# Column-tiled transposes and denominator sums, and a searched order with a lead for dense work, in a two-layer attention and MLP kernel

## The chip, the core and the metric

The kernel runs on one core of a Trainium2 chip. The core has five engines with an instruction stream each: PE (matrix products, from SBUF into PSUM), ACT (activations), DVE and POOL (elementwise work), SP (here it only issues transfers). They meet through semaphores alone. The metric is the device time of one execution in microseconds (us). Times "before" are the median of 8 runs.

## What is computed

Four blocks in a row, each with its input added to its output: attention A, mixer and MLP B, attention A, mixer and MLP B. Both A use the same weights, and so do both B. There are 2048 tokens of 512 values in bf16. Attention has 32 heads of 16 values, which share one key and one value head. Cut to what matters:

```python
def _A_ref(x, wq, wk, wv, wo):            # x: (1, 2048, 512), H = 32, Dh = 16
    q = (x @ wq).reshape(B, S, H, Dh).transpose(0, 2, 1, 3)
    k = x @ wk
    v = x @ wv
    p = softmax(einsum("bhqd,bkd->bhqk", q, k) * Dh ** -0.5)
    o = einsum("bhqk,bkd->bhqd", p, v)
    return o.transpose(0, 2, 1, 3).reshape(B, S, H * Dh) @ wo

def _B_ref(x, w1, w2, w3, w4):            # w3: (512, 1792), w4: (1792, 512)
    h = gelu(layernorm(x) @ w1)
    # the four quarters of h are moved along the tokens by +1, -1, +2, -2
    x1 = x + shifted(h) @ w2
    return x1 + gelu(layernorm(x1) @ w3) @ w4

x = A_x
x = x + _A_ref(layernorm(x), ...)
x = x + _B_ref(layernorm(x), ...)
x = x + _A_ref(layernorm(x), ...)
x = x + _B_ref(layernorm(x), ...)
```

## The kernel before

The tokens are 16 tiles of 128. A layer (A and B together) takes them in chunks of four tiles as queries; the last four of layer 1 are two chunks of two. A chunk's attention is eight blocks `b` of four heads, a block is 16 key tiles `kb`, and each of these is cut into two halves of two heads. With the two short chunks counted in steps of two key tiles, a layer has 1024 such halves, of 128 x 1024 scores each.

**Halves and their two ways.** PE forms the scores (L1072, QT and KT, on array tiles of 32 rows, one for each head). Then either ACT takes the exponential (L1116, `declare_unit`: 1024 columns from two PSUM banks into EA; two such slots of banks take turns), or the half is "given" to DVE and POOL (`declare_pair`): DVE turns the scores into the bits of a bf16 power of two (L1137, J), and two further integer additions (L1147, JK, on POOL or DVE) give three terms whose weighted sum approximates the exponential. PE adds EA @ VP, or three products with J, JK and the scaled VD, in one PSUM bank ACC (L1196, `declare_pv`). A column of ones in VP collects the denominators.

**The end of a block** (`block_end`): DVE copies ACC to ACCF (L1230); PE picks the denominators out of it with SELC (L1238, `fz`: 128 x 128 of ACCF against 4 columns, four times for 512 queries), DVE takes reciprocals (L1245), PE spreads them with IDENT (L1253, `fx`), DVE multiplies (L1259, OS), and SP moves the result to OT in eight transfers (L1282).

**The end of a chunk** (`chunk_end`): output projection (`outproj`), layer norms with rows in ZR, transposes of 128 x 128 on PE (L868, `across`; then one copy at L877), first mixer product (`mixer_in`) with its gelu on ACT (L1457, GP), second (`mix`), the MLP's first product (`mlp`, copies at L1532) with its gelu (L1537, G), and its second (`mlp_out`). A tile whose mixing needs tokens of the next chunk is left to that chunk, so MLP groups of layer 0 are tiles 0-2, 3-6, 7-10, 11-13 and 14-15. At the passage from layer 0 to 1 each finished tile gives keys and values of layer 1 (`kv`), on which the first chunk of layer 1 waits; it therefore takes the key tiles in three stretches (below 6, below 11, the rest).

**What sets the order.** Nothing here is a loop over engines. `Plan` is a list scheduler that runs while the program is built: each operation has a duration, a priority and its inputs, and `run` places operations on model times; `emit` writes the resulting order, with semaphore waits, into the program. On the chip every engine follows that order. Side work (all that is not attention) is released no faster than `PACE` allows: an operation's `ready` is at least its `entry`, which moves on by each operation's PE time. `MARGIN` is what the planner adds when PE waits for another engine. `SWITCH` is what it charges when PE changes among three kinds of work: "Q" (scores, 32-row tiles), "P" (32-column tiles) and "F" (full array: transposes, `fz`, values). `filler` puts products of ONES and NIL on PE when its activity in a window is low. `assign` decides when a half is given to DVE and POOL.

Eight of the planner's numbers (`RULES`) change along the way: each stretch of 12.5 us takes one of 16 rows of `MOODS`, and the string `TEMPER` names the row of each stretch. It has been found by a search over built orders.

Of the kernel before, what the change touches and what calls it, by code (L numbers as in the profile page):

```python
# [25 lines left out]

class Op:
    __slots__ = ("eng", "emit", "preds", "npend", "succ", "dur", "prio", "seq", "ready", "start",
                 "end", "take", "give", "dma", "out", "pos", "sem", "vc", "side", "placed", "pe", "feeds", "port", "parts", "after")


class Plan:
# [6 lines left out]

    DRAIN = {"ACT": 0.15, "DVE": 0.085, "POOL": 0.0}  # L40
    SELF = 0.035
    MARGIN = 0.09
    SWITCH = 0.103
    WAVE = 0.006
    WINDOW = 3.4133
# [2 lines left out]
    KEEP = 0.55  # L48
# [8 lines left out]
    PATIENCE = 3.0  # L57
    SLACK = -0.1
    DMA_LATE = 2.5
    NEAR_FILL = 0  # L60
    STICK = -1
    CLOSE = 2.5
# [38 lines left out]
    def op(self, eng, emit, reads=(), writes=(), dur=0.1, prio=None, take=None, give=None,  # L101
           dma=0, out=False, side=True, pe=None, port=False, parts=1, after=0.0):
        o = Op()
        o.eng, o.emit, o.dur, o.take, o.give, o.dma, o.out, o.side = \
            eng, emit, dur, take, give, dma, out, side
        o.pe = pe
        o.port = port
        o.parts = parts
        o.after = after
        o.feeds = None  # L110
        o.seq = len(self.ops)
        o.prio = self.base if prio is None else prio
        o.succ = []
        o.placed = False
        o.start = o.end = None
        o.pos = None
        preds = set()
        for t in reads:
            r = self.res.get(t)
            if r is not None and r[0] is not None:  # L120
                preds.add(r[0])
        for t in writes:
            r = self.res.get(t)
            if r is not None:
                if r[0] is not None:
                    preds.add(r[0])
                preds.update(r[1])
        for t in reads:
            self.res.setdefault(t, [None, []])[1].append(o)
        for t in writes:  # L130
            self.res[t] = [o, []]
        o.preds = preds
        for t in writes:
            if isinstance(t, Late):
                if take is None:
                    t.gates += [p for p in preds if p not in t.ops]
                t.ops.append(o)
        o.ready = self.now
        if self.pace is not None and side:
            if pe is not None:  # L140
                self.release += pe[1] * self.pace / 2400.0
                if take is not None:
                    self.entry = self.release
            o.ready = max(o.ready, self.entry)
        n = 0
        for p in preds:
            if p.placed:
                o.ready = max(o.ready, self._after(p, o))
            else:
                p.succ.append(o)  # L150
                n += 1
        o.npend = n
        self.ops.append(o)
        self.left += 1
        if n == 0:
            self._push(o)
        return o
# [35 lines left out]

    def _push(self, o):
        self.heap[o.eng].append(o)
        heapq.heappush(self.events, o.ready)

    def _pick(self, eng, t, dense=False):
# [13 lines left out]
        best = None  # L212
        bank = None
        for o in h:
            if o.ready > t + 1e-9:
                continue
            if eng == "ACT" and self.closing and o.side and not all(u.placed for u in self.units[-4:]):
                continue
            if joins and (o.pe[0] != self.pe_kind or self.begin(o, t) > t + 1e-9):
                continue  # L220
            if limit and o.prio > 0:
                end = self.run_end(o, t)
                if (not joins or end > self.pe_end + 0.02) and \
                        any(end + (self.SWITCH if o.pe[0] != "Q" else 0.0) > x for x in limit):
                    continue
            if pressing and self.run_end(o, t) > self.pe_end + 0.02:
                continue
            key = (low.get(o, o.prio), o.seq)
            if self.CLOSE and eng == "PE" and o.prio > 2 and o not in low and o.take is None:
                key = (self.CLOSE, o.seq)  # L230
            if stick and o.prio > 2 and o.pe[0] == self.pe_kind and not any(self.run_end(o, t) + self.SWITCH > x for x in due):
                key = (self.STICK, o.seq)
            if o in pinned:
                key = (self.PINNED, o.seq)
            if best is not None and key > best[0]:
                continue
            k = None
            if o.take is not None:
                if not all(p.placed and (p.end <= t + 1e-9 or p.eng == "PE") for p in o.take.gates):
                    continue  # L240
                margin = self.MARGIN if o.side else self.LAT["PE"]
                for i, (ft, b) in enumerate(self.pool):
                    if ft + margin <= t + 1e-9 and (k is None or ft < self.pool[k][0]):
                        k = i
                if k is None or o.prio > 2 and len(self.pool) <= self.SPARE and self.attach is not None and not self.loose:
                    continue
            best = (key, o)
            bank = k
        if best is None:
            return None  # L250
        o = best[1]
# [65 lines left out]
        return self.free_at["DVE"] - self.now + sum(o.dur for o in self.heap["DVE"] if o.prio <= 2)  # L317

    def backlog(self):
        return sum(o.dur for o in self.heap["DVE"] if o.side and o.ready <= self.now + 0.5)  # L320

    def _place(self, o, t):
        o.start = t
        o.placed = True
        if o.port and o.eng == "POOL" and o.dur > 0.5:
            x = self.order["DVE"][-1] if self.order["DVE"] else None
# [3 lines left out]
        o.pos = len(self.order[o.eng])  # L330
        self.order[o.eng].append(o)
        if o.dma:
            s = max(t + 0.61 * (o.parts - 1) + 1.4, self.dma_free)
            o.end = s + o.dma / 330e3 + 0.6
            self.dma_free = s + o.dma / 330e3
            self.free_at[o.eng] = t + 0.63 * o.parts
        elif o.eng == "PE":
            self.roll(t)
            kind, stream, act = o.pe[0:3]
# [2 lines left out]
            end = t + stream / f + (self.WAVE * ((stream + 511) // 512) if kind == "P" else 0.0)  # L342
# [170 lines left out]
def mm(n, k=1):  # L513
    return ("F", max(n, 60) * k, n * k)


def tiled(n, k=1):
    return ("P", n * k, n * k, range(4))
# [6 lines left out]
class Kernel:  # L525
# [16 lines left out]
    ADDS = 4  # L542
# [10 lines left out]
    MAX_PAIRS = 2  # L553
    BACKLOG = 1
    FAR = 20
    FREE = 2
    LONELY = 3
    SOON = 0.45
    QUEUE = 0.7

    STRETCH = 12.5
    RULES = ("KEEP", "PATIENCE", "BACKLOG", "LONELY", "SOON", "QUEUE", "MAX_PAIRS", "ADDS")
    MOODS = (
        (0.55, 3.0, 1.0, 3.0, 0.45, 0.7, 2, 4),
        (0.53, 2.5, 0.8, 3.0, 0.45, 0.7, 2, 5),
        (0.57, 3.5, 1.2, 3.3, 0.45, 0.7, 2, 4),
        (0.52, 3.0, 1.5, 2.0, 0.6, 0.7, 2, 5),
        (0.55, 2.0, 1.0, 3.0, 0.3, 1.0, 2, 4),
        (0.55, 4.0, 0.7, 4.0, 0.45, 0.5, 2, 4),
        (0.55, 3.0, 1.0, 3.0, 0.45, 0.7, 1, 4),  # L570
        (0.55, 3.0, 1.5, 2.5, 0.6, 1.0, 3, 5),
        (0.60, 3.0, 0.6, 3.0, 0.2, 0.4, 2, 4),
        (0.50, 2.7, 1.1, 2.8, 0.5, 0.8, 2, 4),
        (0.55, 3.0, 2.0, 1.5, 0.45, 0.7, 2, 3),
        (0.55, 1.0, 1.0, 3.0, 0.45, 0.7, 2, 4),
        (0.55, 3.0, 1.0, 3.0, 0.45, 0.7, 2, 5),
        (0.55, 3.0, 1.0, 3.0, 0.45, 0.7, 2, 3),
        (0.55, 3.0, 1.5, 3.0, 0.7, 1.2, 3, 6),
        (0.57, 2.0, 1.0, 2.0, 0.45, 1.0, 3, 4),
    )  # L580
    TEMPER = "8033ee39ee377177e2fc0e03ec3fe7470c0ad17fee0e5df7ee7330e00050000a42037e4ce5591f07513f43f3fee2df192097e373cc00f03c4"

    def __init__(self, nc, ins, out):
        self.stretch = -1
# [271 lines left out]
    def across(self, tiles, dst, dtags, base=None, prio=None, eng="DVE"):  # L856
# [5 lines left out]
        for hd in range(2):  # L862
            def fpe(e, hd=hd):
                ins = None
                for dc in (2 * hd, 2 * hd + 1):
                    for i, tb in enumerate(tiles):
                        x = (dc * n + i) * 128
                        ins = e.transpose(self.PBH[:, L.bank, x:x + 128], rows[:, tb % 4, dc * 128:(dc + 1) * 128],  # L868
                                          self.IDENT)
                return ins  # L870
            op("PE", fpe, reads=[(name, tb % 4) for tb in tiles] + [("ID",)], writes=[L], pe=mm(128, 2 * n),
               prio=prio, take=L if hd == 0 else None)
        src = lambda: self.shaped(self.PBH[:, L.bank, 0:512 * n], [4, n * 128])
        if eng == "ACT":
# [329 lines left out]
    def block_end(self, la, c, b, end):  # L1204
# [30 lines left out]
        def fz(e):  # L1235
            ins = None
            for q in range(nq):
                ins = e.matmul(self.PB[:, L.bank, 4 * q:4 * q + 4], lhsT=acc[:, q * 128:(q + 1) * 128],  # L1238
                               rhs=self.SELC, start=True, stop=True)
            return ins  # L1240
        op("PE", fz, reads=am + [("SELC",)], writes=[L], pe=("F", 60 * nq, 4 * nq), prio=fin, take=L)

        def frec(e):
            with self.nc.allow_low_precision("the reciprocals feed a bf16 matmul"):
# [359 lines left out]
```

## Time and profile before

| | |
|---|---|
| median of 8 runs (lowest, highest) | 1501.86 us (1501.41, 1502.61) |
| the profiled execution | 1501.62 us, of which span 1499.8 us |
| granted clock of PE | 1.000 |
| exponentials on ACT (L1116) | 1430, 1315.7 us busy |
| halves on DVE and POOL | 618 (1236 J of 681 ns; JK: 1014 on POOL, 222 on DVE) |
| transposes (L868) | 384 |
| denominator products (L1238) | 256 |
| filler matmuls (ONES, NIL, L671) | 636 of 396 ns, four of them side by side |
| ACT table loads | 30 of 1.283 us |
| weight and input transfers | 7.9 MB read; queues busy 4.9% of 16 engines |

A row of the groups gives line, engine, operation, what is written from what, the count, busy time and mean length, and after the second bar the engine's idle time before such instructions with what ended it. [...]what a matmul costs its engine is read from the distance of the starts in the timeline. PE's 98% is such a sum of overlapping records, not a measure of how much of PE is used.

### The profile page before, as it was taken

To read this page: it belongs to the slowest core of one execution; us is meant where nothing else is said; L and a number is where in the kernel's file an instruction comes from. 1 tells how busy PE (TensorE), PEld (TensorE's weight loads), DVE (VectorE), ACT (ScalarE), POOL (GpSimd) and SP (SyncE) were. 2 spreads that over 40 slices of the span, in tenths; PEclk is the share of its full clock that TensorE was granted. 3 is DMA by queue.
4 is the path that set the end of the run, shared out by engine and by line. 5 is a ranking of instruction groups with operands and counts; after the bars stand their busy time and mean duration, and the time that the engine had idled before them with its cause. 6 is when DMAs were issued, how large, how long until landed. Compare 5 with 4: busy or idle time off the path is not lost.

```text
span 1499.8 us, 62760 instructions
## 1 busy us (share of the span) xinstructions
PE 1476.8 (98%) x28277; PEld 653.8 (44%) x28277; DVE 1327.5 (89%) x2397; ACT 1429.3 (95%) x1520; POOL 1210.9 (81%) x1275
## 2 busy tenths in 40 slices
PE   9999999999999999999999999999999999999999
PEld 4343343444443444444354334344443344555565
DVE  8999999998999999999886799998799998988973
ACT  7999999999999999999959999999999999999952
POOL 2999999997998887998833799889889898887941
PEclk9999999999999999999999999999999999999999
DMA  6100100001000000100000000010000000000000
GB/s 213 29 7 4 20 6 6 6 4 20 7 6 4 6 5 6 19 4 2 2 3 3 2 7 13 6 19 5 13 14 6 6 6 13 6 19 10 9 14 24
DMA packets 32141, 21.49 MB, mean 14 GB/s; under 512 B 12672, under 2 KB 31360, under 8 KB 31872
## 3 DMA queue, kind: packets, MB, share of 16 engines
q1 hardware_dynamic: 31872, 17.47, 4.9%
q8 instruction: 221, 3.62, 1.0%
q14 instruction: 48, 0.39, 0.1%
HBM read 7.90 MB, written 2.10 MB: 7 GB/s over the span
## 4 chain that ended last, share of the span: by engine, by line
ACT 71%; PE 24%; DVE 3%; POOL 1%; issue 0%; DMA 0%; POOLq 0%
ACT EA L1116 68%; PE PB L671 10%; PE PB L1072 6%; PE PB L1196 6%; ACT G L1537 1%; DVE J L1137 1%; POOL JK L1147 1%; ACT L1116 1%; PE PB L868 1%; ACT GP L1457 1%; DVE JK L1147 0%; PE PB L925 0%; ACT L1457 0%; ACT L1537 0%; DVE ST L786 0%; DVE G L1532 0%
## 5 line engine op out<-in xcount | busy, mean ns | idle before, releaser
L1116 ACT ACTIVATE EA<-PB 128x1024 bf16<-128x1024 f32 x1430 | 1315.7, 1150 | 5.4 <-PE PB L1072 3.1
L1147 POOL TENSOR_SCALAR JK<-J 128x1024 uint16<-128x1024 uint16 x1014 | 1074.3, 1060 | 169.0 <-DVE J L1137 84.5
L1137 DVE TENSOR_SCALAR J<-PB 128x512 uint16<-128x512 f32 x1236 | 794.5, 681 | 75.2 <-PE PB L1072 70.3
L1072 PE MATMUL PB<-QT,KT 32*128 32x512 bf16 (+1 forms) x4608 | 610.2, 359 | 13.1 <-ACT EA L1116 6.2
L1196 PE MATMUL PB<-EA,VP 128*32 128x256 bf16 (+1 forms) x6448 | 370.0, 263 | 1.4 <-DVE ACCF L1230 1.0
L1072 PEld LDWEIGHTS PB<-QT,KT 32*128 32x128 bf16 x4608 | 163.0, 91 | 377.3 <-ACT EA L1116 301.0
L1196 PE MATMUL PB<-JK,VD 128*32 128x256 bf16 (+1 forms) x5536 | 318.2, 266 | 2.2 <-POOL JK L1147 1.1
L1196 PEld LDWEIGHTS PB<-EA,VP 128*32 128x32 bf16 x6448 | 154.7, 95 | 121.2 <-issue 93.9
L1196 PEld LDWEIGHTS PB<-JK,VD 128*32 128x32 bf16 x5536 | 126.7, 94 | 149.1 <-issue 93.0
L1196 PE MATMUL PB<-J,VD 128*32 128x256 bf16 (+1 forms) x2768 | 175.3, 264 | 0.2 <-DVE J L1137 0.2
L671 PE MATMUL PB<-ZT,W 128*32 128x512 bf16 (+2 forms) x2816 | 167.6, 342 | 0.7 <-DVE J L1137 0.2
L1147 DVE TENSOR_SCALAR JK<-J 128x1024 uint16<-128x1024 uint16 x222 | 141.4, 643 | 3.2 <-PE PB L1196 1.0
L671 PE MATMUL PB<-W,G 128*32 128x512 bf16 x1624 | 103.0, 380 | 0.1
L1196 PEld LDWEIGHTS PB<-J,VD 128*32 128x32 bf16 x2768 | 67.8, 95 | 42.1 <-issue 34.3
L1532 DVE CAST G<-PB 128x512 bf16<-128x512 f32 (+2 forms) x126 | 71.9, 580 | 15.3 <-PE PB L671 14.3
L671 PEld LDWEIGHTS PB<-ZT,W 128*32 128x32 bf16 x2816 | 65.0, 96 | 33.1 <-issue 16.8
L1537 ACT ACTIVATE G<-G 128x1792 bf16<-128x1792 bf16 x29 | 47.0, 1686 | 32.7 <-DVE G L1532 32.6
L806 POOL TENSOR_TENSOR SM<-SM,MH 128x2 f32<-128x2 f32 (+1 forms) x69 | 49.1, 715 | 21.2 <-DVE SM L808 10.0
L671 PE MATMUL PB<-ONES,NIL 128*32 128x512 bf16 x636 | 57.8, 396 | 0.1
L671 PEld LDWEIGHTS PB<-W,G 128*32 128x32 bf16 x1624 | 41.3, 96 | 34.4 <-issue 9.2
L1259 DVE TENSOR_TENSOR OS<-ACCF,PB 128x512 bf16<-128x512 bf16 (+1 forms) x72 | 44.6, 620 | 7.5 <-PE PB L1253 7.4
L1513 POOL TENSOR_TENSOR X<-Y,X 128x512 f32<-128x512 bf16 x32 | 37.6, 1180 | 9.7 <-DVE Y L1495 7.8
(108 smaller groups left out, 837.0 us busy)
## 6 DMA issues: line engine op xcount, KB each, us to landing
OT<-OS SPq DMA_DIRECT2D x424, 8.0 KB, 1.8
W<-in_B_w_dram SPq DMA_DIRECT2D x2, 1792.0 KB, 14.5
X<-in_A_x_dram SPq DMA_DIRECT2D x8, 256.0 KB, 4.9
QT<-QS SPq DMA_DIRECT2D x32, 64.0 KB, 2.4
out_dram<-OUTB SPq DMA_DIRECT2D x16, 128.0 KB, 1.7
OT<-OS SPq DMA_DIRECT2D x104, 4.0 KB, 2.2
W<-in_B_w_dram SPq DMA_DIRECT2D x2, 512.0 KB, 8.9
WQ<-in_A_wq_dram SPq DMA_DIRECT2D x1, 512.0 KB, 4.4
```

Source lines behind the costliest of these rows:

```text
L671: ins = e.matmul(self.PB[32 * g:32 * g + 32, bank, 0:n], lhsT=lhsT[:, 32 * g:32 * g + 32], rhs=rhs, start=start, stop=stop, tile_position= ...
L806: op("POOL", lambda e: e.tensor_tensor(out=out, in0=src, in1=self.MH[:, 0, a:b], op=ALU.pow), reads=tags + [("MH",)], writes=tg(r), dur=0. ...
L868: ins = e.transpose(self.PBH[:, L.bank, x:x + 128], rows[:, tb % 4, dc * 128:(dc + 1) * 128], self.IDENT)
L1072: ins = e.matmul(self.PB[:, bank, j * n:(j + 1) * n], lhsT=self.KT[32 * h:32 * h + 32, la, (kb + j) * 128:(kb + j + 1) * 128], rhs=self.QT ...
L1116: o = q.feeds = op("ACT", lambda e: e.activation(self.EA[:, ea, :, :], self.PB[:, b0:b0 + 2, :], ACTF.Exp, scale=0.25), writes=bk + [("EA" ...
L1137: o = op("DVE", lambda e, i=i, L=L: e.tensor_scalar(out=J[:, i * 512:(i + 1) * 512], in0=self.PB[:, L.bank, :], scalar1=128 * LOG2E * 0.25 ...
L1147: x = op(eng, lambda e, k=k, r=r: e.tensor_scalar(out=self.JK[:, r, :], in0=J, scalar1=float(self.STEPS[k]), scalar2=1.0, op0=ALU.add, op1 ...
L1196: ins = e.matmul(self.PB[32 * x:32 * x + 32, self.ACC, p * hw:p * hw + hw], lhsT=v[:, la, kb + j, :], rhs=ap[:, i, j * w + u * hw:j * w + ...
L1259: op("DVE", lambda e: e.tensor_tensor(out=osm, in0=acc, in1=self.PB[:, M.bank, 0:n], op=ALU.mult), reads=am, writes=[M] + om, dur=t_ps(n), ...
L1513: op("POOL", lambda e, tb=tb: e.tensor_tensor(out=self.X32[:, tb, :], in0=self.Y[:, tb % 6, :], in1=self.X32[:, tb, :], op=ALU.add), reads ...
L1532: op("DVE", lambda e, f=f, L=L: e.tensor_copy(self.G2[:, f, 0:n], self.PB[:, L.bank, 0:n]), writes=[L] + [(x, f, i) for x in ("G2", "GE") ...
L1537: op("ACT", lambda e, i=i: e.activation(self.G2[:, :, i * 128:(i + 1) * 128], self.G2[:, :, i * 128:(i + 1) * 128], ACTF.Gelu_apprx_tanh), ...
```

## The change

- The transposes of `across` and the products of `fz` are issued as four column tiles: each 128-column left operand is cut into four of 32 columns, and each part writes its own 32 PSUM partitions. There are four times as many instructions, and the planner counts them as kind "P", like most other products. `fz` is priced at 100 columns for each 128 queries.
- `entry` leaves `ready`: an operation of the side work can be picked when its `entry` is no more than `EAGER` ahead. `EAGER` is a ninth rule of the table (-15 to 20 us; 0 in most rows), and rows 10 and 13 are changed in other rules too.
- The planner takes 0.7 us for each transfer that SP issues, in place of 0.61 and 0.63.
- `MARGIN` is 0.15, not 0.09.
- `TEMPER` is another string.

```diff
-    MARGIN = 0.09
+    MARGIN = 0.15
...
+    EAGER = 0.0
+    ISSUE = 0.7
...
         o.ready = self.now
+        o.entry = 0.0
         if self.pace is not None and side:
...
-            o.ready = max(o.ready, self.entry)
+            o.entry = self.entry
...
         self.heap[o.eng].append(o)
+        if o.entry > self.now:
+            heapq.heappush(self.events, o.entry)
         heapq.heappush(self.events, o.ready)
...
-            if o.ready > t + 1e-9:
+            if o.ready > t + 1e-9 or o.entry > t + self.EAGER:
...
-        return sum(o.dur for o in self.heap["DVE"] if o.side and o.ready <= self.now + 0.5)
+        return sum(o.dur for o in self.heap["DVE"] if o.side and max(o.ready, o.entry - self.EAGER) <= self.now + 0.5)
...
-            s = max(t + 0.61 * (o.parts - 1) + 1.4, self.dma_free)
+            s = max(t + self.ISSUE * (o.parts - 1) + 1.4, self.dma_free)
...
-            self.free_at[o.eng] = t + 0.63 * o.parts
+            self.free_at[o.eng] = t + self.ISSUE * o.parts
...
-    RULES = ("KEEP", "PATIENCE", "BACKLOG", "LONELY", "SOON", "QUEUE", "MAX_PAIRS", "ADDS")
+    RULES = ("KEEP", "PATIENCE", "BACKLOG", "LONELY", "SOON", "QUEUE", "MAX_PAIRS", "ADDS", "EAGER")
...
-        (0.57, 3.5, 1.2, 3.3, 0.45, 0.7, 2, 4),
-        (0.52, 3.0, 1.5, 2.0, 0.6, 0.7, 2, 5),
...
-        (0.55, 3.0, 2.0, 1.5, 0.45, 0.7, 2, 3),
+        (0.57, 3.5, 1.2, 3.3, 0.45, 0.7, 2, 4, 8.0),
+        (0.52, 3.0, 1.5, 2.0, 0.6, 0.7, 2, 5, -6.0),
...
+        (0.55, 3.0, 1.0, 3.0, 0.45, 0.7, 2, 4, 20.0),
...
-    TEMPER = "8033ee39ee377177e2fc0e03ec3fe7470c0ad17fee0e5df7ee7330e00050000a42037e4ce5591f07513f43f3fee2df192097e373cc00f03c4"
+    TEMPER = "0004c7ec07f77e4f907027ef07eeee79fc406e0770e7473e37722cc100f0b580559f773c3777120e4e54ee2fe471e1217c7e4070c38e21c731"
...
-                        ins = e.transpose(self.PBH[:, L.bank, x:x + 128], rows[:, tb % 4, dc * 128:(dc + 1) * 128],
-                                          self.IDENT)
+                        for g in range(4):
+                            y = dc * 128 + 32 * g
+                            ins = e.transpose(self.PBH[32 * g:32 * g + 32, L.bank, x:x + 128],
+                                              rows[:, tb % 4, y:y + 32], self.IDENT, tile_position=(0, 32 * g))
                 return ins
-            op("PE", fpe, reads=[(name, tb % 4) for tb in tiles] + [("ID",)], writes=[L], pe=mm(128, 2 * n),
+            op("PE", fpe, reads=[(name, tb % 4) for tb in tiles] + [("ID",)], writes=[L], pe=tiled(128, 2 * n),
...
-                ins = e.matmul(self.PB[:, L.bank, 4 * q:4 * q + 4], lhsT=acc[:, q * 128:(q + 1) * 128],
-                               rhs=self.SELC, start=True, stop=True)
+                for g in range(4):
+                    y = q * 128 + 32 * g
+                    ins = e.matmul(self.PB[32 * g:32 * g + 32, L.bank, 4 * q:4 * q + 4], lhsT=acc[:, y:y + 32],
+                                   rhs=self.SELC, start=True, stop=True, tile_position=(0, 32 * g))
             return ins
-        op("PE", fz, reads=am + [("SELC",)], writes=[L], pe=("F", 60 * nq, 4 * nq), prio=fin, take=L)
+        op("PE", fz, reads=am + [("SELC",)], writes=[L], pe=("P", 100 * nq, 4 * nq, range(4)), prio=fin, take=L)
```

## The prediction

> **What bounds the kernel now.** Read first the busy times and the chain of waits on the page: ACT is the last engine for 71% of the span, PE for 24%, and no transfer is in the chain.
>
> ```profile
> PE 1476.8 (98%) x28277; PEld 653.8 (44%) x28277; DVE 1327.5 (89%) x2397; ACT 1429.3 (95%) x1520; POOL 1210.9 (81%) x1275
> ACT 71%; PE 24%; DVE 3%; POOL 1%; issue 0%; DMA 0%; POOLq 0%
> ```
>
> ACT was busy 1429.3 of 1499.8 us, so only 70.5 us of its time can be won without giving it less work. The second view is the timeline of ACT alone, which shows where those 70.5 us lie. Its columns are start, length, instruction, and in brackets the idle time before it with its cause.
>
> ```profile
> 33.97 201.77 ACT L1116 ACTIVATE EA<-PB 128x1024 bf16<-128x1024 f32 x220 [0.62 <-PE PB L1072]
> ...
> 754.00 1.91 ACT L1457 ACTIVATE GP<-GP 128x2048 bf16<-128x2048 bf16 x1
> ...
> 759.55 6.46 ACT L1537 ACTIVATE G<-G 128x1792 bf16<-128x1792 bf16 x4
> ...
> 786.22 4.87 ACT L1537 ACTIVATE G<-G 128x1792 bf16<-128x1792 bf16 x3 [15.66 <-DVE G L1532]
> ...
> 794.83 10.46 ACT L1116 ACTIVATE EA<-PB 128x1024 bf16<-128x1024 f32 x11 [0.49 <-PE PB L1072]
> 806.80 16.61 ACT L1116 ACTIVATE EA<-PB 128x1024 bf16<-128x1024 f32 x18 [1.52 <-PE PB L1196]
> ```
>
> The first row is what most of the kernel looks like: 220 exponentials in 201.77 us, 0.917 us each, without a gap. The others are the passage from layer 0 to layer 1. There ACT stands 15.66 + 0.49 + 1.52 = 17.7 us. Up to 33.97 us another 7.7 us are lost, and from the last exponential (ended at 1437.06 us) to the end of the span a tail of 62.7 us runs on PE. Everywhere else ACT's gaps sum to about 1 us. So the end can move by four things alone: ACT's work, the head, the passage, the tail. The third view, the timeline of PE in the passage, says why ACT stands.
>
> ```profile
> 758.49 0.39 PE L1072 MATMUL PB<-QT,KT 32*128 32x512 bf16 x2
> 758.80 2.78 PE L671 MATMUL PB<-W,GP 128*32 128x512 bf16 x48
> 761.41 4.92 PE L671 MATMUL PB<-W,G 128*32 128x512 bf16 x88
> ...
> 781.23 4.07 PE L671 MATMUL PB<-ZT,W 128*32 128x384 bf16 x96
> 785.24 0.84 PE L868 MATMUL PB<-IDENT,QS 128*128 128x128 bf16 x12
> ```
>
> After the scores at 758.49 PE writes no scores until 787.94: it works off in one piece what two tile groups left, and ACT has nothing in hand but gelus that wait for it.
>
> **Part 1, the new order (table, lead, planned transfers).** The planner writes each engine's order into the program, so both orders can be counted. The counts: exponentials 1430 to 1433; pairs of score tiles on DVE and POOL 618 to 615; ACT table loads 30 to 28; filler matmuls 636 to 612. Layer 0 has 706 exponentials on ACT in both, with the same gelus and loads, so up to there nothing moves.
> ACT's work: 3 x 0.917 = +2.75 us, and two loads of 1.283 us less (the page's L1116 loads) = -2.57. Sum **+0.2 us**. DVE loses 6 J (681 ns) and 6 JK (643 ns), 8 us off the path.
>
> The passage. Before, ACT's order is: 769 exponentials, the mixer gelu GP, 1 exponential, four MLP gelus (chunk 2), 2 exponentials, three gelus (first part of chunk 3), then 31. After: 748, the four gelus, GP directly behind, 29 exponentials, the three gelus, 36. Chunk 2's first MLP product is done by exponential 747, not 770, and PE's one block becomes two. I price a block from rows: two 512-wide dots are 0.43 us (the 88 matmuls from 761.41 to 766.26 are 11 such: 4.85 us with a switch), two 384-wide 0.325 (the 96 from 781.23 to 785.24 are 12 such: 4.0), a P.V group 0.11, a scores pair with its switch 0.32. As a check, the old block has 6 mix and 28 MLP-out halves (34 x 0.43), 28 halves of 384 (9.1), six transpose ops (1.1), seven P.V groups (0.8) and four switches (0.4): 26.0 us, and the trace has 758.80 to 785.24, 26.4.
> - First new block, behind exponential 750's scores: 0.3 + six P.V 0.66 + 8 mixer halves 3.44 + 18 MLP-out 7.74 + 4 mix 1.72 + 0.4 = 14.3 us, and 0.3 for the next scores. ACT meanwhile has load 1.28, four gelus 6.46, GP 1.91, load 1.28, two exponentials 1.83 = 12.8. ACT stands 1.9 us. GP needs the mixer's casts 5.2 us into the block and comes at 7.7, so it does not wait.
> - Between the blocks 26 exponentials (23.8 us of ACT) have about 23 us of PE work: no gap.
> - Second block, behind exponential 777's scores: 0.32 + 0.33 + 5 MLP-out 2.15 + 22 halves of 384 7.15 + 0.55 for the last cast = 10.5 us; ACT holds two exponentials and a load, 3.1. ACT stands 7.4.
> - The last stretch (fillers, third group) I leave near its old value, 2.0 to 1.3.
> Idle 10.6 for 17.7: **-7.1 us**. Were all PE work pushed against ACT's, without the bank of the gelus, it would be 12.5 (-5); if PE also runs ahead between the blocks, 8.5 (-9).
>
> Waits that the new order adds: behind the four gelus on ACT now stand GP and all exponentials; if GP is late, PE waits for the score banks too. The time from layer 0's last exponential to GP shrinks from 59 to 46 us. Before, POOL's chain for the first two tiles took 717.08 to 725.5, with four JK of 1.04 to 1.23 between its steps; after, its eight steps stand together, so some 4.4 us shorter, and the moved transposes come about 10 us behind the outproj, for a chain of some 7. Enough.
> SP: 626 transfers in both; per issue the trace has 5.92/8 = 0.74 us. The waits view has one wait of DVE for a DMA, 1.5 us at the first load, and none for OT or QT, so planned issue times cost or win nothing by themselves (0 to -1). Out stores and QT copies trade places in layer 1, without a waiter in that view.
>
> **Part 2, transposes and sums in four column tiles.** Runs of one array shape change 3009 times before, 2880 after. One change costs 0.10 us (P.V to P.V 0.12, P.V to scores 0.22 start to start). -129 x 0.10 = -13 us of PE. A transpose op becomes 16 small matmuls of exactly the shape of the L1253 row, which stream as long as four full ones did. For the sums the nearest row is the same:
>
> ```profile
> L1253 PE MATMUL PB<-IDENT,RZ 128*32 128x128 bf16 x1024 | 29.0, 220 | 0.0
> L1238 PE MATMUL PB<-SELC,ACCF 128*128 128x4 bf16 x256 | 17.4, 168 | 0.0
> ```
>
> Sixteen of them ran 403.46 to 403.79, 0.23 us without the switch, 14 ns each. The old sums of four took 0.18 with a switch, 0.08 without. So 64 blocks cost 64 x 0.13 = +8 us. Against it speaks the Trainium skill, TensorEngine Tiling, section Instruction Overhead: about 60 cycles for each matmul however small, and no tiling taken from a dimension that is small already; here it is 4. At the 2.4 GHz that page TensorE: Matmul & The Clock Gate states, that is an estimated 25 ns, 0.40 a block, 64 x 0.32 = +20 us. By the row the part, with 6 fillers fewer (-1.3), gives PE -6 us; by the rule +6. I take the row: same shape, same engine, and it has 0.23, not 0.40. Either lies off the path where ACT has no gap: with shared rows counted once, PE's rows sum to about 0.93 of ACT's time outside the passage, in both orders (at worst 1.02 per 50 exponentials before, 0.97 after), and two exponentials (1.8 us) of score banks hide a block of 0.4. If the cover were gone, -6 to +6 us would show.
> In the tail PE sets the end. After: one MLP half (0.43) and one P.V group (0.11) fewer, five runs of full-array work lose two switches each (0.8 to 1.0), sums +0.06: **-1.3 us** (0 to -2). The head has the same transposes and two fillers more, still before data: 0 (+-0.7).
>
> **Sum.** +0.2 - 7.1 - 1.3 = -8.2: span 1491.6. The profiled execution took 1501.62, 1.8 around its span, and 0.24 under the median: 1491.6 + 1.8 + 0.2 = **1493.6 us**.
>
> **Rivals.**
> 1. The gap stays the same size: the passage is work, not order, and PE's sum there falls only by pairs and switches (7 pairs fewer between exponentials 750 and 800, 3 us). Then +0.2 - 3 - 1 = 1498. For it: PE had no gap from 753 to 785. Against: 11 us of gelus now lie over PE's first block. 0.15.
> 2. The gain is larger: transposes and rearranged stages also clear the head (7.7 us) and the gap before the second block: -14, 1488. Nothing in the head's order says so. 0.12.
> 3. Slower: a producer is late at a moved transpose or at GP. PE works in order, so scores queue behind; beyond 1.8 us of bank ACT stands. Before, POOL's chain with JK between took 14 us from the second tile's outproj to its transpose; after, some chunks leave 10. If the chain stays long, 4 - 1.8 = 2.2 us at each of 9 chunk ends, 20 us: 1493.6 + 20 = 1513; it decides from four ends on. Against: the JK are out of that chain, and the planner leaves 0.15 us where it left 0.09. 0.10.
> 4. The lead and tiles do nothing, the order is a reshuffle: 1501.9, 0.05.
>
> The rest, 0.58, is the forecast. The range takes its bounds and rivals 1 and 2: 1487.5 to 1500.5. From no change a measurement here tells 0.2%, 3 us (1498.9 to 1504.9). Faster 0.81, same 0.08, slower 0.11.
>
> **What would show it.** On ACT's timeline the three gelus' wait falls from 15.66 to 6 to 9, with about 2 us after GP; the last exponential ends near 1430; the tail is 61 us. The L1238 group's blocks start 0.2 to 0.25 apart from what follows; 0.4 would be the rule's price. A wait of ACT for scores, above 1 us and outside the passage, would be rival 3.

## The result, and the profile after

The changed kernel takes 1497.24 us (median of 10 runs, 1496.61 to 1498.63) against 1501.89 us for the kernel before on the same chip: ratio 0.9969, 95% interval 0.9961 to 0.9977. The gain is 4.65 us where 8.3 were forecast. The profiled execution is the longest of the ten, 1498.63 us with a span of 1496.5. A second execution with the same order on PE, ACT, DVE and SP (experiment 3) took 1496.81 us, span 1495.0. It is used beside the first, because it shows how far two executions of one order lie apart.

The page first: two lines that answer to those shown of before.

```profile
PE 1468.2 (98%) x30149; PEld 652.1 (44%) x30149; DVE 1333.3 (89%) x2385; ACT 1429.7 (96%) x1521; POOL 1212.6 (81%) x1275
ACT 61%; PE 30%; DVE 6%; POOL 2%; issue 1%; DMA 0%; SPq 0%
```

ACT has the same work as before (1429.7 for 1429.3 us). PE lost 8.6 us of busy time although it now carries 1872 more matmuls. In the chain of waits PE and DVE gained share, 30 and 6% for 24 and 3: ACT is less alone on the path than it was.

The timeline of ACT alone tells where the time went. Its columns are start, length, instruction, and the idle time before it with its cause.

```profile
9.08 1.01 ACT L882 COPY YT<-PB 128x1024 bf16<-128x1024 bf16 x1 [2.40 <-PE PB L875]
13.23 0.59 ACT L940 CAST KT<-PB 128x512 bf16<-128x512 f32 x1 [3.14 <-PE PB L932]
14.46 5.63 ACT L1123 ACTIVATE EA<-PB 128x1024 bf16<-128x1024 f32 x6 [0.64 <-PE PB L1079]
21.90 5.60 ACT L1123 ACTIVATE EA<-PB 128x1024 bf16<-128x1024 f32 x6 [1.81 <-PE PB L1079]
28.90 6.64 ACT L1123 ACTIVATE EA<-PB 128x1024 bf16<-128x1024 f32 x7 [1.40 <-PE PB L1079]
36.10 212.33 ACT L1123 ACTIVATE EA<-PB 128x1024 bf16<-128x1024 f32 x231 [0.56 <-PE PB L1079]
...
738.76 6.46 ACT L1546 ACTIVATE G<-G 128x1792 bf16<-128x1792 bf16 x4
745.12 1.89 ACT L1466 ACTIVATE GP<-GP 128x2048 bf16<-128x2048 bf16 x1
...
752.59 24.89 ACT L1123 ACTIVATE EA<-PB 128x1024 bf16<-128x1024 f32 x27 [2.33 <-PE PB L1079]
...
787.06 4.87 ACT L1546 ACTIVATE G<-G 128x1792 bf16<-128x1792 bf16 x3 [8.28 <-DVE G L1541]
...
795.60 15.88 ACT L1123 ACTIVATE EA<-PB 128x1024 bf16<-128x1024 f32 x17 [0.42 <-PE PB L1079]
812.52 15.69 ACT L1123 ACTIVATE EA<-PB 128x1024 bf16<-128x1024 f32 x17 [1.03 <-PE PB L1203]
```

In the passage, from 738 us on, the one wait of 15.66 us has become two, 2.33 and 8.28, as the forecast had it (1.9 and 7.4). The new loss is at the top: the waits of 1.81 and 1.40 us at 21.90 and 28.90 stood at 0.56 and 0.38 before. These are the rows of before:

```profile
19.82 7.44 ACT L1116 ACTIVATE EA<-PB 128x1024 bf16<-128x1024 f32 x8 [0.56 <-PE PB L1072]
27.64 5.71 ACT L1116 ACTIVATE EA<-PB 128x1024 bf16<-128x1024 f32 x6 [0.38 <-PE PB L1072]
```

PE's timeline of the kernel after shows both the passage's first block and what happens ahead of those two waits.

```profile
20.41 0.29 PE L875 MATMUL PB<-IDENT,ZR 128*32 128x128 bf16 x6
20.97 0.57 PE L875 MATMUL PB<-IDENT,ZR 128*32 128x128 bf16 x26 [0.28 <-issue]
21.47 0.40 PE L1079 MATMUL PB<-QT,KT 32*128 32x512 bf16 x4
...
26.25 0.61 PE L932 MATMUL PB<-YT,WK 128*32 128x512 bf16 x6
27.72 0.82 PE L932 MATMUL PB<-YT,WK 128*32 128x512 bf16 x10 [0.85 <-issue]
28.47 0.39 PE L1079 MATMUL PB<-QT,KT 32*128 32x512 bf16 x2
...
380.11 0.29 PE L1203 MATMUL PB<-J,VD 128*32 128x256 bf16 x4
380.23 0.25 PE L1247 MATMUL PB<-SELC,ACCF 128*32 128x4 bf16 x16
380.33 0.28 PE L1203 MATMUL PB<-JK,VD 128*32 128x256 bf16 x4
...
738.78 3.63 PE L676 MATMUL PB<-ZT,W 128*32 128x512 bf16 x64
742.23 7.94 PE L676 MATMUL PB<-W,G 128*32 128x512 bf16 x144
750.00 1.90 PE L676 MATMUL PB<-W,GP 128*32 128x512 bf16 x32
```

Twice in the head PE stops in the middle of one operation, after 6 of 32 transposes and after 6 of 16 key products, with "issue" as the cause: no semaphore was awaited. From 738.78 to 751.73 lies the first new block, 64 + 144 + 32 matmuls, eight for each half: the 8 mixer, 18 MLP-out and 4 mix halves that were forecast. The rows at 380 us are read further down.

All of ACT's time adds up to the span, so the account can be closed. Exponentials are the summed lengths of their rows; head is the idle time in rows that start before 40 us, the tail what follows the last exponential.

| us, after less before | forecast | profiled after | same order, second execution |
|---|---|---|---|
| exponentials (1433 for 1430) and two table loads fewer | +0.2 | +3.4 - 2.6 | +2.6 - 2.6 |
| head (7.66 before) | 0 | +3.0 | +2.7 |
| passage (17.67 before) | -7.1 | -5.6 | -5.6 |
| gaps elsewhere (0.95 before) | 0 | 0.0 | -0.4 |
| tail (62.75 before) | -1.3 | -1.45 | -1.4 |
| span | -8.2 | -3.3 | -4.8 |

Two theories for the difference were open. **The fetch theory**: in the head PE's instructions, which come by DMA themselves, arrive late beside the weight loads, because tiled transposes are four times as many instructions. **The order theory**: the new order itself is worse in the head. And a question beside it: which part of the change carries the gain, the tiles, the order, or the lead? The expectations below number their theories each for itself; the text between them uses these names.

### The profile page after: what moved, and what is told of

Its sections match the earlier page's. It is cut to its first block, busy times and chain, and to the rows that moved or that the text cites. A ratio compares the mean times of both kernels' runs of the same rounds, so it can differ in the third digit from the quotient of the medians.

```text
span 1496.5 us, 66501 instructions
## 1 busy us (share of the span) xinstructions
PE 1468.2 (98%) x30149; PEld 652.1 (44%) x30149; DVE 1333.3 (89%) x2385; ACT 1429.7 (96%) x1521; POOL 1212.6 (81%) x1275
## 4 chain that ended last, share of the span: by engine, by line
ACT 61%; PE 30%; DVE 6%; POOL 2%; issue 1%; DMA 0%; SPq 0%
ACT EA L1123 57%; PE PB L1079 10%; PE PB L676 9%; PE PB L1203 9%; DVE J L1144 3%; POOL JK L1154 2%; ACT G L1546 2%; ACT L1123 1%; PE PB L875 1%; DVE ST L791 1%; DVE G L1541 1%; ACT GP L1466 1%; PE PB L932 0%; DMA X<-in_A_x_dram 0%; DVE JK L1154 0%
## 5 line engine op out<-in xcount | busy, mean ns | idle before, releaser
L1123 ACT ACTIVATE EA<-PB 128x1024 bf16<-128x1024 f32 x1433 | 1318.8, 1127 | 9.8 <-PE PB L1079 8.1
L1203 PE MATMUL PB<-EA,VP 128*32 128x256 bf16 (+1 forms) x6460 | 366.3, 263 | 0.7 <-DVE ACCF L1237 0.4
L1203 PE MATMUL PB<-JK,VD 128*32 128x256 bf16 (+1 forms) x5512 | 321.6, 266 | 4.6 <-POOL JK L1154 2.6
L1154 DVE TENSOR_SCALAR JK<-J 128x1024 uint16<-128x1024 uint16 x216 | 152.1, 712 | 2.4 <-PE PB L1203 0.8
L676 PEld LDWEIGHTS PB<-W,G 128*32 128x32 bf16 x1624 | 38.0, 96 | 36.2 <-issue 10.7
L1522 POOL TENSOR_TENSOR X<-Y,X 128x512 f32<-128x512 bf16 x32 | 37.3, 1169 | 11.7 <-DVE Y L1504 10.0
## 6 DMA issues: line engine op xcount, KB each, us to landing
W<-in_B_w_dram SPq DMA_DIRECT2D x2, 1792.0 KB, 14.5
```

The lines of the kernel that those rows point to most:

```text
L676: ins = e.matmul(self.PB[32 * g:32 * g + 32, bank, 0:n], lhsT=lhsT[:, 32 * g:32 * g + 32], rhs=rhs, start=start, stop=stop, tile_position= ...
L1123: o = q.feeds = op("ACT", lambda e: e.activation(self.EA[:, ea, :, :], self.PB[:, b0:b0 + 2, :], ACTF.Exp, scale=0.25), writes=bk + [("EA" ...
L1154: x = op(eng, lambda e, k=k, r=r: e.tensor_scalar(out=self.JK[:, r, :], in0=J, scalar1=float(self.STEPS[k]), scalar2=1.0, op0=ALU.add, op1 ...
L1203: ins = e.matmul(self.PB[32 * x:32 * x + 32, self.ACC, p * hw:p * hw + hw], lhsT=v[:, la, kb + j, :], rhs=ap[:, i, j * w + u * hw:j * w + ...
L1522: op("POOL", lambda e, tb=tb: e.tensor_tensor(out=self.X32[:, tb, :], in0=self.Y[:, tb % 6, :], in1=self.X32[:, tb, :], op=ALU.add), reads ...
```

## The experiments

### 1 and 2. Tiles alone, order alone

The order of before with tiled transposes and sums:

```diff
-                ins = e.matmul(self.PB[:, L.bank, 4 * q:4 * q + 4], lhsT=acc[:, q * 128:(q + 1) * 128],
-                               rhs=self.SELC, start=True, stop=True)
+                for g in range(4):
+                    y = q * 128 + 32 * g
+                    ins = e.matmul(self.PB[32 * g:32 * g + 32, L.bank, 4 * q:4 * q + 4], lhsT=acc[:, y:y + 32],
+                                   rhs=self.SELC, start=True, stop=True, tile_position=(0, 32 * g))
...
```

> The order of before, planned as before; only the instructions of the transposes and of the denominator sums are cut into four column tiles. Runs of one array shape fall from 3010 to 2879. Theory 1 (the order makes the gain in the passage, the tiles only save switches where PE sets the end): tail shorter by about 1 us, passage by 0.5 to 1, head 0 to +1: 1500 to 1501 us. Rival A (the tiles are the gain): 1497 to 1498. Rival B (each small product costs about 25 ns): the sums' blocks start 0.4 us before what follows and the time is 1502 or more.

And the kernel after with both put back to full-array instructions, the planned order unchanged (the same diff with its signs turned, applied to after).

> The order of after, with transposes and sums as full-array instructions again. Runs of one array shape rise from 2881 to 3099, 22 us of switches on PE that the plan does not know. Theory 1: only the tail (+1 to +1.5) and the passage (+1) show them, the rest lies under ACT: about 1499.5 us. Rival A (the tiles are the gain): 1501 to 1502 or more, with new waits of ACT for scores outside the passage. If the longer head of after comes from its many small transposes, the head's idle time falls from 10.7 to about 8 us here and the time is about 1498.

Measured: tiles in the old order 1501.99 us (ratio to before 1.0001, 0.9992 to 1.0010); the new order with full-array instructions 1501.49 (0.9998, 0.9990 to 1.0007). Neither part alone gains anything that can be told from zero; together they gain 4.65. The tiled instructions in the old order raised the head from 7.66 to 9.10 us of idle time, and with it came pauses of the same kind as in the kernel after. PE's timeline of that kernel:

```profile
13.63 0.46 PE L870 MATMUL PB<-IDENT,ZR 128*32 128x128 bf16 x18
14.74 0.40 PE L870 MATMUL PB<-IDENT,ZR 128*32 128x128 bf16 x14 [0.65 <-issue]
...
26.59 0.39 PE L671 MATMUL PB<-YT,WQ 128*32 128x512 bf16 x2
27.68 0.61 PE L671 MATMUL PB<-YT,WQ 128*32 128x512 bf16 x6 [0.69 <-issue]
```

The order alone has its passage at 12.40 us, as good as after, and a shorter head, 8.83. Its tail is 1.0 us longer than that of after (62.3 for 61.3). Most of what it loses lies in a place that no list of gaps shows. The group of the exponentials on the page of after and then of experiment 2 (after the bar: busy time, mean length):

```profile
L1123 ACT ACTIVATE EA<-PB 128x1024 bf16<-128x1024 f32 x1433 | 1318.8, 1127 | 9.8 <-PE PB L1079 8.1
```

```profile
L1121 ACT ACTIVATE EA<-PB 128x1024 bf16<-128x1024 f32 x1433 | 1321.9, 1109 | 8.8 <-PE PB L1077 6.6
```

The same 1433 exponentials take 3.1 us more, with a *shorter* mean length. Their records overlap: 1433 of 1127 ns are 1615 us, and together they cover 1318.8. In experiment 2 they overlap less (by 0.19 us on average, for 0.21), so they cover more. The distance from one start to the next, taken from the single records of the trace, has a median of 0.904 us in both kernels. What grew are the long distances: 190 above 0.93 us for 162, which hold 16.0 us in all above 0.917, for 11.7. It is a wait cut into pieces too short for the timeline, which gives a gap a row of its own from 0.15 us on. PE's busy time rose by 10 us (1468.2 to 1478.2); that PE's later scores make these pieces fits this, but the pieces carry no cause in the trace.

### 3. The lead set to zero

```diff
         (0.57, 2.0, 1.0, 2.0, 0.45, 1.0, 3, 4, 0.0),
+        (0.55, 3.0, 1.0, 3.0, 0.45, 0.7, 2, 4, 0.0),
...
+        (0.57, 3.5, 1.2, 3.3, 0.45, 0.7, 2, 4, 0.0),
...
```

The table gets 16 further rows, copies of the old ones with 0.0 as the ninth number, and `TEMPER` names the copy wherever it named the old row.

> The ninth rule is 0 in every row, all else as after. In the built program the orders of PE, ACT, DVE and SP are those of after; on POOL one scaling of a tile's rows moves by ten places. Theory 1 (the earlier MLP product comes from the search and the other planner numbers, not from the lead): 1497.2 us, within 0.5. Rival (the lead brings the gain): 1499 or more.

Measured: 1497.21 us (0.9970, 0.9959 to 0.9981). With the lead at zero the planner writes the same order on PE, ACT, DVE and SP; on POOL one operation of the mixer moves by ten places. So in this table the ninth rule does nothing. What moved the passage is the search (with the planner's new prices), not the lead.

### 4. Weight loads held to 40 us

```diff
     def emit(self):
         nc = self.nc
+        gate = next(o for o in self.order["PE"] if o.start >= 40.0)
+        loads = [o for o in self.order["SP"] if o.dma >= 524288 and o.prio >= 5]
...
+        for i, o in enumerate(loads):
+            o.preds.add(gate)
+            o.start = gate.start + 0.001 * (i + 1)
```

> After, but the five loads of WO and of the four MLP weights wait until PE has come about 40 us into the plan; all orders on PE, ACT, DVE and POOL as after. Theory 2 (in the head PE waits for its own instructions, which come by DMA beside 5.2 MB of weights; after has more of them): the pauses inside PE's blocks at 20 and 26 us go, the head's idle time on ACT falls from 10.7 to 8 or less, and the time is about 1495 us. Rival (the head is longer because of its order): 1497.2, head 10 to 11 us.

Measured: 1504.01 us (1.0015, 1.0006 to 1.0023), slower. The head did fall, from 10.67 to 8.57 us, and the waits of 1.81 and 1.40 became 1.31 and 0.16. But the loads moved into the way of something else. Two rows of this kernel's timeline:

```profile
61.38 0.69 DVE L996 CAST QS<-PB 128x512 bf16<-128x512 f32 x1 [6.78 <-DMA QT<-QS]
...
63.97 1.02 ACT L1129 ACTIVATE EA<-PB 128x1024 bf16<-128x1024 f32 x1 [6.92 <-PE PB L1085]
```

DVE waits 6.78 us for a QT copy that reads QS before it may overwrite QS; the copy was issued at 54 us, behind 5.2 MB of weights. PE's query products wait for DVE, and ACT stands 6.92 us. The place for the loads must lie behind the copies of 64 to 70 us.

### 5 and 6. Weight loads held to 74 us, in after and in before

The same edit with 74.0 for 40.0.

> The kernel after, with the five weight loads of WO and W held until a matmul planned at 74 us, behind the QT copies of 64 to 70 us, so that they leave the head and meet no copy that something waits for. Theory 1 (in the head PE waits for its own instructions, which come by DMA and queue behind the weights; tiled transposes made them more): ACT's idle before 40 us falls from 10.7 to about 8.6, as when the loads were held to 40 us, no gap at 64 us, and the kernel takes 1497.2 - 2 = about 1495.2 us. Theory 2 (the longer head comes from the new order alone): 10.7 stays, 1497.2. Theory 3 (the weights only move the stall to 75 to 90 us): head 8.6, a new ACT gap of about 2 us behind 75 us, 1497.

> The kernel before, with the same hold of the five weight loads. PE has no wait for instructions of its own in the head of the kernel before (its waits there are for DVE and ACT), so theory 1 (the larger number of instructions in the head makes the stall) expects no change: head idle 7.7, 1501.9 us. If the weights slow any head (theory 4), the head falls here too by 1 to 2 us: 1500 to 1501.

Measured: after with held loads 1495.62 us (0.9957, 0.9944 to 0.9969), before with held loads 1501.84 beside 1501.88 (0.9999, 0.9990 to 1.0008). The fetch theory holds on both sides: the head of after falls to 8.35 with no gap behind 74 us, that of before stays (7.60 for 7.66). PE's and then ACT's timeline of the kernel after with held loads:

```profile
19.83 0.63 PE L881 MATMUL PB<-IDENT,ZR 128*32 128x128 bf16 x32
...
25.17 1.05 PE L938 MATMUL PB<-YT,WK 128*32 128x512 bf16 x16
```

```profile
20.82 5.61 ACT L1129 ACTIVATE EA<-PB 128x1024 bf16<-128x1024 f32 x6 [1.31 <-PE PB L1085]
26.58 6.64 ACT L1129 ACTIVATE EA<-PB 128x1024 bf16<-128x1024 f32 x7 [0.16 <-PE PB L1085]
```

The operations that were torn in two run whole. The DMA view, asked in steps of half a microsecond, gives the reason. The instruction queue's packets (16 KB each) began at 12.0, 18.0 and 25.0 us in after, and at 10.5, 14.5 and 20.0 with the weights out of the way: the second and third came 3.5 and 5 us later beside the weights, of which PE's own lag in the program explains about 1. From 8 to 24 us the DMA engines' busy share is 1.08 in after (packets overlap) and 0.20 with the loads held.

The single records of the trace tie the pauses to these packets. Six traces have twelve pauses (after and experiments 1, 3, 7, 8 and 9), and each of them stands after 223, 351 or 479 matmuls, wherever in an operation that falls. These places are 128 matmuls apart, which with their weight loads is 256 instructions. In each of the twelve PE goes on 1.3 to 1.5 us after the end of a packet. From start to start the two pauses of after are 0.50 and 1.23 us (the 0.28 and 0.85 of the rows count from the modelled end of the record ahead). The two waits of ACT behind them sum to 3.21 us, 1.74 more than the two with held loads. In before the second packet came late too, at 21.5 us for 18.5 with held loads, but PE did not stop there: by 24 us it had come only to its 313th matmul, where after had come to its 421st. In what way the loads hold a packet up, the traces do not show.

On the page the queue has grown by 14 packets; the line of before, then that of after:

```profile
q8 instruction: 221, 3.62, 1.0%
```

```profile
q8 instruction: 235, 3.85, 1.1%
```

1872 more matmuls, each with its weight load, are 3744 instructions. The Trainium skill (Runtime: NRT & Kernel Launch, Instruction fetch mechanics) says that an engine's instructions are refilled in blocks of 16 KiB, which are 256 instructions: 3744 / 256 = 14.6, and the trace has 14 packets more. (The 221 packets of before hold 221 x 256 = 56576 instructions; its 28277 matmuls and as many weight loads are 56554.) The page also says that the price of crossing a block is mostly hidden. Over most of this run it is. In the head it is not, with pauses of 0.28 and 0.85 us by the rows; the measurement decides.

### 7. Only the sums put back to the full array

The sums' part of the diff of experiment 2.

> The kernel after with only the denominator sums back as full-array matmuls; transposes stay in tiles, the order stays. With both undone the time was 1501.5. Theory 1 (array switches cost ACT time in small waits between exponentials, whoever causes them): the sums' part is about half of that, 1499.3, with exponentials summing to 1321 instead of 1319.3. Theory 2 (the transposes carry it all, sums were a loss of PE time of 8 us for small products): 1497 or less. Theory 3 (sums carry it): 1501.5.

Measured: 1498.97 us (0.9980, 0.9971 to 0.9989), exponentials 1320.7 us. Tiled sums are thus worth some 1.7 us. Tiled transposes bring the other 2.5 of experiment 2, and that is net of what they cost in the head (10.11 us of idle time here, 8.83 there). PE's busy time rose by 4.4 us, where the forecast had held that tiled sums would *cost* 8 us, before switches. The same block as in the rows at 380 us above, in this kernel:

```profile
379.68 0.29 PE L1203 MATMUL PB<-J,VD 128*32 128x256 bf16 x4
379.91 0.25 PE L1245 MATMUL PB<-SELC,ACCF 128*128 128x4 bf16 x4
380.09 0.29 PE L1203 MATMUL PB<-JK,VD 128*32 128x256 bf16 x4
```

From the product ahead to the product behind it is 0.41 us with four full-array sums, and 0.22 with sixteen in tiles. In the single records of the kernel after, the sixteen start in four rounds of four that are 25 ns apart, 0.10 us in all; the four full-array products of this kernel's block start within 0.09 us. So the products themselves cost about the same either way. What the tiles save are the two changes of the array's shape around a block, 0.19 us here, about twice the 0.10 that the forecast read for one change. Over all 72 blocks (56 of sixteen products, 16 of eight) the distance falls from 0.39 to 0.24 us on average, 10.7 us in all.

### 8. Half of the second block left out

This kernel makes one dot instead of two for each half of the first MLP product of tiles 11 to 13 of layer 0.

```diff
-                    for dc in (2 * h, 2 * h + 1):
+                    for dc in (2 * h, 2 * h + 1) if la or len(tiles) != 3 or tiles[0] == 0 else (3 * h,):
```

> The kernel after, leaving out half of the first MLP product of layer 0's tile group 11 to 13 (each of its 28 halves makes one dot of 384 columns instead of two), so PE's second block in the passage is shorter by some 20 to 22 halves x 0.163 us = 3.4 us. Theory 1 (that block sets ACT's wait one for one): the wait before the three gelus falls from 8.28 to about 4.9 and the kernel takes 1493.8. Theory 2 (something else, casts on DVE or the banks, sets the wait): it stays above 7, and the kernel within 1 us of 1497.2.

Measured: 1494.94 us (0.9953, 0.9940 to 0.9967); the wait fell from 8.28 to 6.39, not to 4.9. The block does set the wait, but not alone. The timeline of PE in this kernel:

```profile
780.29 2.00 PE L676 MATMUL PB<-ZT,W 128*32 128x384 bf16 x32
782.85 0.51 PE L676 MATMUL PB<-ZT,W 128*32 128x384 bf16 x8 [0.55 <-DVE G L1541]
```

PE now stands for DVE's cast, because DVE has an addition and a norm's statistics of 0.68 us each among the last casts. In after PE has no pause there, but DVE has none either from 782.13 us on. The part of PE's block ahead of its last ten halves fell from 6.17 to 4.44 us, 1.7 of the 1.9 by which ACT's wait fell. The last ten halves, with half the work, took 3.09 us for 3.25: there DVE is the limit.

### 9, 10 and 11. The head from the other side

Experiment 9 leaves the loads where they were and takes the instructions away instead: the first eight transpose operations are full-array again.

```diff
+                self.turned = getattr(self, "turned", 0) + 1
...
+                        if self.turned <= 8:
+                            ins = e.transpose(self.PBH[:, L.bank, x:x + 128], rows[:, tb % 4, dc * 128:(dc + 1) * 128],
+                                              self.IDENT)
+                            continue
                         for g in range(4):
```

> The kernel after with the first 8 transpose operations (all that lie before 35 us) as full-array matmuls, the other 56 and the sums in tiles; weight loads where they were. This takes 192 matmuls and their loads, 384 instructions, out of the head and 1 to 2 us of array switches per operation do not matter there. Theory 1 (the head's extra wait is PE's instructions coming late beside the weight loads, and the tiled transposes brought it on): PE's pauses labelled issue inside the blocks at 20 and 27 us go, the head falls from 10.1-10.7 to 8.4-8.9, and the kernel takes about 1495.6, as with the weight loads held. Theory 2 (the order alone, or only the loads): head above 10, 1497.2.

Experiment 10 is experiment 1 with the loads held to 74 us, experiment 11 is 5 and 9 together.

> The order of the kernel before with all transposes and sums in tiles (1502.0 with the loads at the start, head 9.1), now with the five weight loads held to 74 us. Theory 1: the head returns to 7.6-7.7 as before, and the kernel takes 1502.0 - 1.4 = 1500.6, so tiles without their price in the head are worth 1.3 us in the old order. If the head stays at 9.1 and the time at 1502.0, the pauses inside its blocks have another cause than the weight loads.

> The kernel after with both: weight loads held to 74 us and the first 8 transpose operations as full-array matmuls. Theory 1: both edits cure the same pauses, so together they give no more than one: head 8.3 to 8.8, 1495.6 +- 0.4. If they cure different things, the gains add: head about 6.5 to 7, 1494.

| | median, us | ratio to before (95%) | head idle | pauses of PE matmuls labelled issue |
|---|---|---|---|---|
| 9: fewer instructions in the head | 1496.27 | 0.9961 (0.9948 to 0.9973) | 9.17 | 0.23 |
| 10: tiles, old order, loads held | 1501.21 | 0.9994 (0.9985 to 1.0003) | 7.61 | none |
| 11: both head edits | 1495.70 | 0.9957 (0.9944 to 0.9969) | 8.61 | none |

The two edits don't add: 11 is at 5's time, so both cure the same thing. Experiment 9 gave most of it, with one pause left: ACT's waits from its seventh exponential to 30 us sum to 1.73 us, for 3.21 in after and 1.47 in experiment 5. Experiment 10 brought the old order's head back from 9.10 to 7.61, as the fetch theory said. Its median is 0.8 us under that of experiment 1; each against the before measured beside it (1502.24 and 1501.85), the difference is 1.2, where 1.4 was forecast. Its interval runs from 2.3 us ahead of before to 0.5 behind, so tiles in the old order stay unseparated from zero.

## Why the forecast was right or wrong, step by step

**The result lies in the range, 3.6 us above the value.** The passage was to carry the gain and did shrink, by 5.6 us; one term of the sum that was set at nothing was 2.7 to 3.0 us. The time alone would speak for rival 1, whose 1498 us is nearer: it is ACT's timeline that decides between the two.

**"The head has the same transposes and two fillers more, still before data: 0 (+-0.7)": this is the step that failed.** It counted the head's work in operations. In instructions it is larger: between 8 and 24 us PE has 364 matmuls instead of 252 although it is behind by then, and their packets go over the DMA engines that bring 5.2 MB of weights. Of the extra 2.7 to 3.0 us, 2.1 to 2.3 go when the loads are held (10.40 or 10.67 to 8.35). The remaining 0.75 (8.35 against 7.60 with held loads) stays in every kernel of the new order, tiled or not: the wait behind the first six exponentials is 1.18 to 1.31 us in experiments 2, 4, 5, 9 and 11, against 0.56 in before. So the order theory has that share. Rival 2, which let the head gain, had the sign wrong.

**The passage was right in kind, and 1.5 us too good in size.** Forecast 1.9, 7.4 and 1.3; measured 2.33, 8.28 and 1.45. The part that PE's block in front of ACT's gelus plays was tested by experiment 8, up to the point where DVE takes over. Rival 1, the same gap in another order, is out: it let the passage shrink by 3 us, and it shrank by 5.6.

**The tail**: -1.3 forecast, -1.4 measured; the tiles alone shortened it by 0.7 us (experiment 1), the order alone by 0.4 (experiment 2). **ACT's work**: the counts were right; the exponentials' spacing differs by 0.8 us between two executions of one order, which is the noise of this term.

**"Against it speaks" the rule of 60 cycles: the row was nearer, and still too dear.** The forecast took 0.23 us a block from a row that it called the same shape, but that row has 128 columns to stream, where the sums have 4; against it stood 0.40, an estimate from the rule of the Trainium skill (TensorEngine Tiling (Array Packing), Instruction Overhead). Measured: 0.10. The estimate of 25 ns is what the trace has, but for a round of four tiles at once; the forecast had put sixteen one behind the other. And the page warns of tiles taken from a dimension that is small already, while these are taken from the 128 columns of the left operand. In the forecast's own terms, without switches, 64 blocks then cost 64 x (0.10 - 0.08) = +1.3 us in place of +8. The error fell on PE's sum: forecast -6 us. PE's busy time fell by 8.6, a sum of overlapping records that can only roughly be set beside it.

**"Either lies off the path where ACT has no gap": wrong for the new order.** Without the tiles PE's busy time is 10 us longer, and 3.1 us appear between exponentials. The part that was priced at nothing on the path is worth 5.4 to 5.9 us in the new order once the head is cured (1501.49 less 1495.62; 0.5 of it may be the held loads, since experiment 2 has its loads at the start and a head of 8.83 for 8.35). In the old order it is about 1 (1501.21 for 1502.24), not separated from zero. So the order alone, credited with 7.1 us, gained 0.4 (experiment 2). The new order was planned with the tiles' cheaper prices, and its reserve is smaller by what they save. That explanation fits the four times, but how the planner spent the saving was not traced.

**"The new order (table, lead, planned transfers)" credited three things at once.** The lead, as the ninth rule sets it, has no part in it (experiment 3). The larger `MARGIN` and planned issue times were not tried alone, since a planner with any one of its prices changed writes another order, for which the table was not searched.

**Rival 3**, a late producer, asked for a wait of ACT for scores above 1 us outside the passage. Such waits are there, 1.81 and 1.40 us, but in the head and from PE's own instructions, not from POOL's chain at a chunk's end. From 40 us to the passage, and behind it, gaps sum to 0.95 us.

**The best version that computes the whole** is experiment 5: the change with the weight loads held behind the second QT copies, 1495.62 us, faster than both kernels.

## What to carry to other kernels

Splitting an operation into small tiles multiplies instructions, and instructions are fetched: count them in any stretch where the DMA engines are full, and look for rows torn in two with "issue" as the cause. Moving a transfer cures one queue and can block another, so look for the next copy that somebody waits for before choosing its place. A schedule and the prices it was planned with are one change: test each part in both the old and the new order, because either alone can be worth nothing.

## What the runs showed of the hardware

- Small products in column tiles run side by side: sixteen of 128 x 32 against 4 columns start in four rounds 25 ns apart. With no change of the array's shape around them a block takes 0.22 us from the product ahead to the one behind, where four full-array products with their two changes take 0.41.
- PE takes its instructions in packets of 256. Beside the weight loads packets began 3.5 and 5 us later than without them, and PE stopped after 351 and 479 matmuls, in the middle of an operation, until 1.5 us after a packet's end.
- A wait can hide in the mean length: exponentials of 1127 ns mean became 1109 ns while the time that they cover grew by 3.1 us.
